# A planned two-layer transformer kernel: the planner counts the SBUF port shared by VectorE and GpSimd, the set-up is reordered, and the two-tile mixer matmuls go in four columns

## The chip, the cores and the metric

The kernel runs on one core of a Trainium2 chip. The metric is the device time of one execution in microseconds (us). Before the change the median of three runs is 1062.91 us (1060.59 to 1063.03). The engines are called as the profile calls them: PE is TensorE's matmul, PEld its weight load, DVE is VectorE, ACT is ScalarE, POOL is GpSimd, and SP is SyncE, which issues most DMAs.

## The reference, cut to what matters

There are 2048 tokens of width 448. Two layers, with the same weights, run one after the other; each adds an attention block and then a mixer block to x.

```python
def _A_ref(x, wqkv, wo):          # 16 heads of width 28
    qkv = (x @ wqkv) ...          # q, k, v
    p = _softmax(q @ k.T * Dh ** -0.5, axis=-1)
    return (p @ v) ... @ wo

def _B_ref(x, w1, w2, w3, w4):
    h = _gelu(_layernorm(x) @ w1)
    hs = (four quarters of h's columns, shifted by 1, 1, 2, 2 tokens) @ w2
    x1 = x + hs
    return x1 + _gelu(_layernorm(x1) @ w3) @ w4   # w3: 448 x 1792

x = A_x
for layer in range(2):
    x = x + _A_ref(_layernorm(x), A_wqkv, A_wo)
    x = x + _B_ref(_layernorm(x), B_w1, B_w2, B_w3, B_w4)
```

## The kernel before

**A static plan.** The order of instructions on each engine is not written by hand. Generators such as k_proj, q_proj, d_chain, t_norm, t_mixA and t_mixB yield operations, each with an engine, an assumed duration, and the tiles that it reads and writes. Sched.run simulates the engines with these durations and picks, again and again, the operation that can start first; priorities (the RANK table, the number given to spawn) decide between operations that compete for PE or DVE. The result is a fixed order on every engine, in which semaphores carry the dependences. The chip keeps the order and not the times: if an instruction takes longer on the chip than in the plan, what stands behind it on its engine waits.

**Attention.** Scores are computed in blocks of 128 keys by 512 columns (four tiles of queries for one head, or two tiles of keys for two tiles of queries). The queries are cut into chunks, CHUNKS: three of four tiles and two of two tiles in each layer; ORDER gives the pieces of the keys in which each chunk is worked through, and four groups g of four heads each run through every piece. One such pass is a segment, and ("segstart", n) is the signal that segment n begins. The scores of three blocks and of two blocks alternate in PSUM banks 0 to 2 and 3 and 4, and one ACT instruction (L1564) exponentiates three or two blocks into PT. PV, the product with v, accumulates in bank 5 (L777). Over both layers there are 2048 blocks.

**Blocks on DVE.** Some blocks bypass ACT: d_first (L1408) takes the scores out of PSUM on DVE, and d_chain makes the exponential there with a polynomial in four more instructions (L1435, L1437, L1439, L1442). t_scores looks for such a block a few rows ahead (DLO to DHI rows, or RLO to RHI for a block that takes the third bank of a unit) if a share of FTH of the planned PE time was filler (D_RATE), or if DVE's planned load is below DTH (R_RATE), if the buffers are free, and if the segment has so far taken fewer than rate x 4 x (row + 1). The rates are per layer and chunk.

**Norms.** t_norm scales the output of attention. One way goes through DRAM (three DMAs: rT, rscr, fb) and ends in a product on POOL (L1669); the other, where PENORM says so, uses small PE matmuls and ends on DVE (L1691). PENORM holds for the last chunk of layer 1 and for the fourth group of a chunk that is true in PE_NORM.

**Mixer.** t_mixA normalizes, transposes by DMA, multiplies by w1 and applies GELU with a tanh: a square on POOL (L1810), a product on DVE (L1811), tanh on ACT (L1812), a product on DVE (L1813). t_mixB does the shifted product with w2, the second norm and w3; GELU is one large ACT instruction for a group of tiles (L1989), with a table load before and after it. t_w4 multiplies by w4. mm (L777) issues one matmul; mm4 (L786) splits a matmul of up to 128 output rows into four of 32 columns of the array each, side by side. Groups of two tiles have a moving width of 256, and t_mixA and t_mixB choose mm4 only above 300. After the last exp the signal ("tail",) opens all banks, and what is left of the mixer runs to the end.

**Fillers.** Where the plan finds PE idle, keep_pe_busy inserts matmuls of an identity (L2035), which compute nothing that is used. The first may come at 6.0 us of the plan.

**Set-up.** t_load loads x and the weights; t_ln1_first normalizes the first four tiles (L964, L965, L970, L972, L979), transposes them on PE (tr_pe, L1003) and copies them to xT on DVE (L1010) or on ACT (L1011). t_pack spreads the columns of wk (on ACT, L910) and of wq (on POOL, L913, or ACT); t_squares (L921) and t_ratio estimate a ratio of weights, whose square root is a power on POOL (L939) and gives RTN (L940). The first projections k and q (k_proj, q_proj) follow, each with a sum of squares; kmaxc, bcb and bc29 (L1138, L1273, L1275) give the bias that the first q (L1176) needs before the first scores.

Of the kernel before, what the change touches and what calls it, by code (L numbers as in the profile page):

```python
# [184 lines left out]
class Sched:  # L185
# [12 lines left out]
    def __init__(self, P):  # L198
        self.P = P
        self.cur = {e: 0.0 for e in ENGS}  # L200
        self.runq = []
        self.pendq = []
        self.opq = []
        self.waiters = {}
        self.cache = {}
        self.seq = 0
        self.pe_mode = None
        self.act_tab = None
        self.events = set()
        self.evt_t = {}  # L210
        self.busy = {}
        self.res_t = {}
        self.log = []
        self.reserved = set()
        self.clock = 0.0
        self.fill = None
        self.recent = []
        self.fills = []
        self.dead = set("b%d" % i for i in range(8))
        self.bank_of = {("ps", i): "b%d" % i for i in range(8)}  # L220
# [102 lines left out]
    def keep_pe_busy(self, until):  # L323
        if self.fill is None:
            return
        if self.pe_mode is None:
            self.pe_mode = "col4"
            self.cur["pe"] = max(self.cur["pe"], 6.0)
        dur, fn, banks, key, reads = self.fill
        forced = 0  # L330
        while True:
            t = self.cur["pe"]
            self.recent = [x for x in self.recent if x[1] > t - 3.4]
# [3 lines left out]
            if not fits:  # L337
                if used > self.LOW * win - self.LCRED * max(0.0, until - t) or forced >= 2:
                    break
                forced += 1  # L340
            elif used > self.TARGET * self.WIN:
                self.cur["pe"] = t + 0.1
                continue
# [19 lines left out]
            self.pe_mode = "col4"  # L363

# [14 lines left out]
    def run(self):  # L379
        P = self.P  # L380
        while True:
# [22 lines left out]
            for t in self.opq:  # L404
# [15 lines left out]
                for ci, ((eng, dur, fn, kw), ready) in enumerate(hit[2]):  # L420
                    if ci > 0 and (self.cur[eng] > ready + 0.05 or eng in self.reserved):
                        continue
                    start = max(ready, self.cur[eng])
                    if eng == "pe":
# [68 lines left out]
            t_end = start + dur  # L493
            if dma:
                self.cur[eng] = start + kw.get("iss", 0.35)
                t_end = start + kw.get("dma_time", 3.0)
            else:
                self.cur[eng] = t_end
# [26 lines left out]
DPRIO = 2.5  # L525
DST = [('dve', 0.6), ('dve', 0.6), ('dve', 0.34), ('dve', 0.6)]
DSEG = 1
R_RATE = {(0, 0): 0, (0, 1): 0.01, (0, 2): 0, (0, 3): 0, (0, 4): 0, (1, 0): 0, (1, 1): 0.03, (1, 2): 0.01, (1, 3): 0, (1, 4): 0.04}
RLO = 5
RHI = 7  # L530
RPRIO = 1
# [3 lines left out]
DLO = 5  # L535
DHI = 7
# [31 lines left out]
def build_kernel(nc, A_x, A_wqkv, A_wo, B_x, B_w1, B_w2, B_w3, B_w4, out, n_layers=2):  # L568
# [79 lines left out]
    with st:  # L648
# [103 lines left out]
        def op(eng, dur, fn, reads=(), writes=(), **kw):  # L752
            return (eng, dur, fn, list(reads), list(writes), kw)
# [1381 lines left out]
```

## Time and profile before

| what | us |
|---|---|
| runs: median (lowest to highest) | 1062.91 (1060.59 to 1063.03) |
| the profiled execution, whole | 1059.41 |
| the profiled execution, span from first to last instruction | 1057.7 |
| ACT busy in the span | 1001.9 |
| PE busy in the span, of it fillers (L2035) | 983.3, 136.6 |
| DVE busy, POOL busy | 735.8, 327.9 |
| first exp starts (L1564) | 16.95 |
| last exp ends | about 1005 |

The span is that of one profiled execution; the 1.7 us between it and the whole lie before its first and after its last instruction. Times in the timeline count from the start of the span. In a group of instructions the columns are: line, engine, operation, out<-in, shapes, count; then busy time and the mean of one in ns; then the idle time just before them and what ended it. In the table by stretches each engine has its busy time and its number of instructions, followed by PE's granted clock (1.00 is full), the DMA share and GB/s.

### The profile page before, as it was taken

How to read it: one execution, taken by the hardware profiler on the slowest of the kernel's cores; microseconds unless marked ns; L12 is line 12 of the kernel's file. 1: busy time of each engine (PE TensorE's matmuls, PEld its weight loads, DVE VectorE, ACT ScalarE, POOL GpSimd, SP SyncE). 2: the span in 40 equal slices, each digit the busy share in tenths (PEclk: the TensorE clock that was granted, in tenths of full speed). 3: DMA queues.
4: the chain of work that ended last, by engine and by line, in shares of the span. 5: the costliest groups of instructions: out<-in, count | busy, mean ns of one | idle time of the engine just before them, and what ended most of it. 6: DMA issues, size and time to landing. Idle time of an engine off the chain costs nothing.

```text
span 1057.7 us, 34104 instructions
## 1 busy us (share of the span) xinstructions
PE 983.3 (93%) x15301; PEld 400.4 (38%) x15301; DVE 735.8 (70%) x1432; ACT 1001.9 (95%) x907; POOL 327.9 (31%) x510
## 2 busy tenths in 40 slices
PE   6999988889999999999999989898889999899998
PEld 2322333234334344444333233343323333444465
DVE  7787799794378546876377846869778575578651
ACT  7999999999999999999999999999899999999952
POOL 2344021641264014462143201103635230433230
PEclk9999999999999999999999999999999999999999
DMA  4557123111221014220033114313502030121001
GB/s 117 130 130 237 50 62 77 42 37 31 69 47 28 18 33 98 52 43 18 22 82 89 40 42 137 110 51 114 83 12 47 25 59 13 41 60 30 12 11 33
DMA packets 96642, 64.28 MB, mean 61 GB/s; under 512 B 68656, under 2 KB 85376, under 8 KB 96496
## 3 DMA queue, kind: packets, MB, share of 16 engines
q1 hardware_dynamic: 93120, 54.02, 20.3%
q0 software_dynamic: 3376, 8.09, 2.8%
q8 instruction: 120, 1.97, 0.7%
q14 instruction: 26, 0.21, 0.1%
HBM read 28.16 MB, written 16.76 MB: 42 GB/s over the span
## 4 chain that ended last, share of the span: by engine, by line
ACT 55%; PE 26%; DVE 12%; DMA 3%; POOL 3%; issue 1%; SPq 0%; DVEq 0%; POOLq 0%
ACT PT L1564 49%; PE ps L786 14%; PE ps L1326 6%; PE ps L777 5%; ACT h2T L1989 3%; DMA rT<-ub 1%; DVE PD L1442 1%; DVE fb L1435 1%; ACT fb L1812 1%; DMA fb<-rscr 1%; DVE fb L1437 1%; DVE PD L1439 1%; DVE yd L1408 1%; ACT L1989 1%; DVE vaug L1408 1%
## 5 line engine op out<-in xcount | busy, mean ns | idle before, releaser
L1564 ACT ACTIVATE PT<-ps 128x1024 bf16<-128x1024 f32 (+1 forms) x797 | 905.8, 1324 | 14.8 <-PE ps L1326 13.4
L1326 PE MATMUL ps<-qT,kT 32*128 32x512 bf16 (+1 forms) x2560 | 311.9, 341 | 30.6 <-ACT PT L1564 25.0
L777 PE MATMUL ps<-PT,vaug 128*32 128x512 bf16 (+1 forms) x2471 | 250.0, 341 | 1.0 <-DVE ub L1645 0.9
L1326 PEld LDWEIGHTS ps<-qT,kT 32*128 32x128 bf16 x2560 | 80.0, 91 | 306.0 <-ACT PT L1564 261.8
L786 PE MATMUL ps<-xT,w 128*32 128x512 bf16 (+1 forms) x2048 | 154.2, 360 | 2.3 <-DVE PD L1439 1.8
L2035 PE MATMUL ps<-ident 128*32 128x256 bf16 x3068 | 136.6, 275 | 7.8 <-DVE yd L1408 2.5
L777 PEld LDWEIGHTS ps<-PT,vaug 128*32 128x32 bf16 x2471 | 73.9, 95 | 95.4 <-issue 78.3
L2035 PEld LDWEIGHTS ps<-ident 128*32 128x32 bf16 x3068 | 84.3, 96 | 36.6 <-issue 13.8
L786 PE MATMUL ps<-w,h2T 128*32 128x448 bf16 x1288 | 87.2, 361 | 7.8 <-ACT h2T L1989 7.4
L1971 DVE CAST h2T<-ps 128x384 bf16<-128x384 f32 (+1 forms) x84 | 52.3, 623 | 60.3 <-PE ps L786 59.8
L1669 POOL TENSOR_TENSOR otn<-ub,fb 128x512 bf16<-128x512 f32 (+1 forms) x36 | 43.3, 1202 | 145.1 <-DMA fb<-rscr 139.1
L786 PEld LDWEIGHTS ps<-xT,w 128*32 128x32 bf16 x2048 | 55.0, 95 | 49.5 <-issue 25.9
L1810 POOL TENSOR_TENSOR fb<-hT 112x512 f32<-112x512 bf16 (+1 forms) x36 | 37.9, 1056 | 73.3 <-DVE hT L1793 68.7
L1113 POOL TENSOR_TENSOR sq<-kT 128x512 bf16<-128x512 bf16 (+2 forms) x32 | 31.4, 988 | 86.2 <-DVE kT L1127 84.1
L1113 POOL TENSOR_TENSOR sq<-qT 128x512 bf16<-128x512 bf16 x28 | 32.4, 1159 | 77.3 <-DVE qT L1160 69.9
L1408 DVE TENSOR_SCALAR yd<-ps 128x512 int32<-128x512 f32 x53 | 35.8, 681 | 24.7 <-PE ps L1326 24.6
L786 PEld LDWEIGHTS ps<-w,h2T 128*32 128x32 bf16 x1288 | 35.1, 97 | 37.7 <-issue 15.1
L786 PE MATMUL ps<-xT,wq_pad 128*32 128x512 bf16 x512 | 44.4, 395 | 2.4 <-DVE hT L1793 1.9
L786 PE MATMUL ps<-xT,wk_pad 128*32 128x512 bf16 (+1 forms) x512 | 44.2, 377 | 0.0
L1896 POOL TENSOR_TENSOR x_res<-x_res,x1b 128x448 f32<-128x448 f32 x32 | 39.2, 1229 | 14.5 <-DVE xn L984 14.3
L970 POOL TENSOR_SCALAR vpe<-mv 128x1 f32<-128x1 f32 (+2 forms) x21 | 6.7, 318 | 114.5 <-DVE mv L965 114.5
L1885 POOL TENSOR_SCALAR mst<-mv 128x1 f32<-128x1 f32 x32 | 9.1, 288 | 102.2 <-DVE mv L965 101.9
(190 smaller groups left out, 1335.4 us busy)
## 6 DMA issues: line engine op xcount, KB each, us to landing
uscr<-ub SPq DMA_DIRECT2D x28, 256.0 KB
ub<-uscr SPq DMA_DIRECT2D x28, 256.0 KB
fb<-rscr SPq DMA_DIRECT2D x24, 256.0 KB
xnd<-xn SPq DMA_DIRECT2D x28, 128.0 KB, 2.0
x_res<-in_A_x_dram POOLq DMA_DIRECT2D x16, 224.0 KB, 2.7
xd<-x_res SPq DMA_DIRECT2D x16, 224.0 KB, 2.7
x_res<-xd SPq DMA_DIRECT2D x16, 224.0 KB, 4.3
out_dram<-obf SPq DMA_DIRECT2D x16, 112.0 KB
```

What stands on the lines that cost most here:

```text
L777: return lambda e: e.matmul(out=out, lhsT=lhsT, rhs=rhs, start=start, stop=stop, **kw)
L786: r.append(e.matmul(out=out[c:c + w, :], lhsT=lhsT[:, c:c + w], rhs=rhs, start=start, stop=stop, tile_position=(0, c)))
L1113: return op("pool", 0.15 + NW * 0.0018, lambda e: e.tensor_tensor(out=sq[:, si, 0:NW], in0=src, in1=src, op=ALU.mult), reads=rk, writes=[( ...
L1326: yield op("pe", (0.005 + NW * 0.00042) / nc_, lambda e, i=i, kc=kc, j=j, g=g, a=a, NW=NW, bank=bank: e.matmul(out=ps[:, bank, i * NW:(i + ...
L1408: yield op("dve", c_ps(512), lambda e: e.tensor_scalar(out=y, in0=ps[:, bi(bank), :], scalar1=SCALE * L2E * FS, scalar2=-126.0 * FS, op0=A ...
L1564: yield op("act", 0.06 + n * w * 0.000833, lambda e, bk=bk, s0=s0, n=n, w=w: e.activation(out=PT[:, s0:s0 + n, 0:w], in_=ps[:, bk[0]:bk[0] ...
L1669: yield op("pool", 0.2 + NW * 0.0021, lambda e: e.tensor_tensor(out=otn[:, g, 0:NW], in0=u, in1=rb[:, 0:NW], op=ALU.mult), reads=[uk, fk], ...
L1810: yield op("pool", 0.2 + NW * 0.00165, lambda e: e.tensor_tensor(out=f, in0=z, in1=z, op=ALU.mult), reads=hk, writes=[fk])
L1896: yield op("pool", 1.2, lambda e: e.tensor_tensor(out=X, in0=X, in1=X1, op=ALU.add), reads=[xk, ("x1b", s)], writes=[xk], deps=[nop_])
L1971: ev = op("dve", c_ps(m * NW), lambda e, hr=hr, pv=pv: e.tensor_copy(out=hr, in_=pv), reads=[("ps", bi(b))], writes=hk, touch=[b])
L1989: yield op("act", c_act(len(fr_) * NW), lambda e, v=v: e.activation(out=v, in_=v, func=ACT.Gelu_apprx_tanh), reads=allk, writes=allk, tab= ...
L2035: return [e.matmul(out=ps[32 * c:32 * c + 32, bi(b), 0:256].rearrange("p (a n) -> p a n", n=128), lhsT=ident[:, 32 * c:32 * c + 32], rhs=i ...
```

## The change

The planner gets a notion of one port. op and alt mark every operation on POOL, and those on DVE that are given `two=True` (the four of d_chain, the norms L979 and L984, the two products of the tanh GELU, L1299, L1348 and the halo copies), with `port`; when such an operation is placed, after_lock moves its planned start behind the running one on the other engine. This alters planned times and so the order; it adds no instruction. The helper both would allow the square, the norm's product, the GELU square and the residual sum on DVE, except for the keys in POOLED, which now holds all four.

The set-up changes: fillers may start at 0.5 us of the plan, count twice their time before 6 us and are not limited by TARGET before 12 us; the first two parts of wq are packed on ACT and the other two on POOL after the fourth norm; t_ratio is spawned at -1; the copies of tr_pe are on DVE alone; the first k goes out of PSUM on ACT alone.

The two-tile matmuls with w1 and w3 use mm4 (above 200 instead of 300). The tables RANK (all but one entry), Q_LEAD, D_RATE, R_RATE and PE_NORM, and DPRIO, RPRIO, DLO and DHI, have new values. LSEG holds the numbers that stood in the code; GMERGE is empty.

```diff
+        self.port = {"dve": (0.0, 0.0), "pool": (0.0, 0.0)}
...
-            self.cur["pe"] = max(self.cur["pe"], 6.0)
+            self.cur["pe"] = max(self.cur["pe"], WARM)
...
+            dur = self.fill[0] * (2 if t < COLD else 1)
...
-            elif used > self.TARGET * self.WIN:
+            elif t > WARMED and used > self.TARGET * self.WIN:
...
+    def after_lock(self, eng, start, dur):
+        a, b = self.port["pool" if eng == "dve" else "dve"]
+        return max(start, b) if start + dur > a else start
...
+                    if kw.get("port"):
+                        start = self.after_lock(eng, start, dur)
...
+            if kw.get("port"):
+                self.port[eng] = (start, t_end)
...
-DPRIO = 2.5
+DPRIO = 1.5
...
-R_RATE = {(0, 0): 0, (0, 1): 0.01, (0, 2): 0, (0, 3): 0, (0, 4): 0, (1, 0): 0, (1, 1): 0.03, (1, 2): 0.01, (1, 3): 0, (1, 4): 0.04}
+R_RATE = {(0, 0): 0, (0, 1): 0.03, (0, 2): 0.01, (0, 3): 0.02, (0, 4): 0, (1, 0): 0, (1, 1): 0, (1, 2): 0, (1, 3): 0.01, (1, 4): 0}
...
-RPRIO = 1
+RPRIO = 0.5
...
-DLO = 5
-DHI = 7
+DLO = 6
+DHI = 8
...
-Q_LEAD = {(0, 1): 8, (0, 2): 7, (0, 3): 10, (1, 0): 8, (1, 1): 11, (1, 2): 3, (1, 3): 4}
-D_RATE = {(0, 0): 0.1, (0, 1): 0.055, (0, 2): 0.035, (0, 3): 0.03, (0, 4): 0.03, (1, 0): 0.025, (1, 1): 0.095, (1, 2): 0.045, (1, 3): 0.005, (1, 4): 0.045}
-PE_NORM = {(0, 0): False, (0, 1): False, (0, 2): False, (0, 3): False, (0, 4): False, (1, 0): False, (1, 1): False, (1, 2): False, (1, 3): False, (1, 4): True, (1, 5): True}
...
+Q_LEAD = {(0, 1): 10, (0, 2): 5, (0, 3): 6, (1, 0): 4, (1, 1): 8, (1, 2): 5, (1, 3): 9}
+D_RATE = {(0, 0): 0.11, (0, 1): 0.1, (0, 2): 0.07, (0, 3): 0, (0, 4): 0, (1, 0): 0.005, (1, 1): 0.105, (1, 2): 0.03, (1, 3): 0.02, (1, 4): 0}
+PE_NORM = {(0, 0): False, (0, 1): False, (0, 2): False, (0, 3): False, (0, 4): False, (1, 0): False, (1, 1): False, (1, 2): False, (1, 3): True, (1, 4): True}
...
+LSEG = (4, 7, 9)
+POOLED = ('sq', 'otn', 'z2', 'xx')
+GMERGE = {}
+WARM = 0.5
+WARMED = 12.0
+COLD = 6.0
...
         def op(eng, dur, fn, reads=(), writes=(), **kw):
+            if eng == "pool" or (eng == "dve" and kw.pop("two", False)):
+                kw["port"] = True
             return (eng, dur, fn, list(reads), list(writes), kw)
...
-            yield ("spawn", t_ratio(), 0)
+            yield ("spawn", t_ratio(), -1)
...
-                if i == 1:
+                if i == 1 or c < 2:
                     yield op("act", 0.5, lambda e, d_=d_, src=src: e.activation(out=d_, in_=src, func=ACT.Identity),
                              reads=[("pt", 4 * i + c)], writes=[((nm,), c)])
                 else:
+                    if c == 2:
+                        yield ("wait", ("xn1", 3))
...
-                             reads=[("pt", 4 * i + c)], writes=[((nm,), c)],
-                             alt=[alt("act", 0.5, lambda e, d_=d_, src=src: e.activation(out=d_, in_=src, func=ACT.Identity))])
+                             reads=[("pt", 4 * i + c)], writes=[((nm,), c)])
...
+            evacs = [("dve", c_ps2(NW), lambda e: e.tensor_scalar(out=dst, in0=ps[:, bi(b), 0:NW], scalar1=MK, scalar2=None, op0=ALU.add)),
+                     ("act", c_act(NW), lambda e: e.activation(out=dst, in_=ps[:, bi(b), 0:NW], func=ACT.Identity, bias=MK))]
+            if fast and g == 0:
+                evacs = evacs[1:]
...
             yield op(D_[0][0], D_[0][1], lambda e: e.scalar_tensor_tensor(out=q, in0=lo, scalar=E2 / E3 * FS, in1=lo, op0=ALU.add, op1=ALU.mult),
-                     reads=yk, writes=fk, urge=urge)
+                     reads=yk, writes=fk, urge=urge, two=True)
...
-                    yield op("pe", c_mm(NW), (mm4 if NW > 300 else mm)(ps[0:112, bi(b), 0:NW], w1[:, fc, 112 * grp:112 * grp + 112], xv(xt)[:, fc, 0:NW], fc == 0, fc == 3),
-                             reads=[("xT", xt), ("w1",)], writes=[("ps", bi(b))], touch=[b], mode="col4" if NW > 300 else "plain")
+                    yield op("pe", c_mm(NW), (mm4 if NW > 200 else mm)(ps[0:112, bi(b), 0:NW], w1[:, fc, 112 * grp:112 * grp + 112], xv(xt)[:, fc, 0:NW], fc == 0, fc == 3),
+                             reads=[("xT", xt), ("w1",)], writes=[("ps", bi(b))], touch=[b], mode="col4" if NW > 200 else "plain")
```

## The prediction

> **What bounds the kernel now.** I read the page first: the engines' shares, then the chain that ended last.
>
> ```profile
> PE 983.3 (93%) x15301; PEld 400.4 (38%) x15301; DVE 735.8 (70%) x1432; ACT 1001.9 (95%) x907; POOL 327.9 (31%) x510
> ACT 55%; PE 26%; DVE 12%; DMA 3%; POOL 3%; issue 1%; SPq 0%; DVEq 0%; POOLq 0%
> ```
>
> ACT is busy 1001.9 of 1057.7 us, and over half of the chain is ACT. PE's 93% holds 136.6 us of fillers (L2035), so its share misleads. Next, busy time by stretches, to see where ACT's missing 56 us lie.
>
> ```profile
> 0.00:17.00 17.00, 9.94 (x115) 4.55 (x119) 12.34 (x51) 10.64 (x15) 6.33 (x20) 1.00 0.63 180
> ...
> 200.00:300.00 100.00, 91.93 (x1393) 36.41 (x1390) 62.91 (x111) 95.32 (x83) 35.79 (x48) 0.97 0.19 46
> ...
> 700.00:800.00 100.00, 88.92 (x1287) 32.63 (x1281) 83.42 (x140) 94.53 (x87) 42.99 (x55) 1.00 0.32 70
> ...
> 1020.00:1040.00 20.00, 19.98 (x444) 11.85 (x440) 8.84 (x18) 6.87 (x14) 6.06 (x9) 1.00 0.06 20
> ```
>
> The columns of busy time are PE, PEld, DVE, ACT, POOL. Three stages: a set-up of 17 us before the first exp; about 988 us in which ACT runs exps; and, from 1005 us, when the last exp ends, a tail of 52.7 us in which PE is full and ACT waits for it. In the middle ACT's gaps over 0.15 us, added from the timeline, come to 15.0 us, most in the second and third stretch above.
>
> Third, the groups by shape, for the price of an exp.
>
> ```profile
> L1564 ACT ACTIVATE PT<-ps 128x1536 bf16<-128x1536 f32 x380 | 587.7, 1547 | 11.1 <-PE ps L1326 9.7
> L1564 ACT ACTIVATE PT<-ps 128x1024 bf16<-128x1024 f32 x416 | 460.7, 1122 | 3.8 <-PE ps L1326 3.7
> ```
>
> Five blocks cost 1547 + 1122 = 2669 ns of ACT: 0.534 us each. ACT does 380 x 3 + 416 x 2 + 1 = 1973 of the 2048 blocks; the other 75 go through DVE (L1408: 53 + 22).
>
> Last, the timelines of the set-up and of one mid gap.
>
> ```profile
> 9.63 0.58 ACT L1011 ACTIVATE xT<-ps 128x512 bf16<-128x512 bf16 x1
> 10.42 1.90 PE L786 MATMUL ps<-xT,wk_pad 128*32 128x512 bf16 x16
> 11.68 1.01 POOL L939 TENSOR_TENSOR sc<-sc,halfs 128x4 f32<-128x4 f32 x1 [1.11 <-DVE sc L938]
> 13.67 0.16 DVE L940 TENSOR_SCALAR sc<-sc 128x4 f32<-128x4 f32 x1
> 15.37 1.04 PE L786 MATMUL ps<-xT,wk_pad 128*32 128x512 bf16 x16
> 16.95 6.88 ACT L1564 ACTIVATE PT<-ps 128x1536 bf16<-128x1536 f32 x6
> ```
>
> The same 16 matmuls take 1.90 us at 10.42 and 1.04 us at 15.37: the first projections run at a slow clock. The last copy of xT waits on ACT until 9.63.
>
> ```profile
> 201.27 2.76 POOL L1669 TENSOR_TENSOR otn<-ub,fb 128x512 bf16<-128x512 f32 x1 [5.24 <-DMA fb<-rscr]
> 205.25 2.11 DVE L1811 SCALAR_TENSOR_TENSOR fb<-fb,hT 112x512 f32<-112x512 f32 x2 [2.35 <-POOL fb L1810]
> 206.79 0.63 ACT L1812 ACTIVATE fb<-fb 112x512 f32<-112x512 f32 x1 [1.60 <-DVE fb L1811]
> 208.02 1.47 PE L786 MATMUL ps<-xT,wq_pad 128*32 128x512 bf16 x12 [1.89 <-DVE hT L1793]
> ```
>
> POOL's product takes 2.76 us while DVE runs (1.27 us when nothing of DVE overlaps), so POOL's next, then DVE's, then ACT's and PE's come late. After PE's idle 1.89 us the granted clock is half for 3.4 us.
>
> **The port.** Dividing each DVE group by whether a POOL instruction overlaps it: L1437 (two SBUF inputs) takes 684 ns alone (46 of 75) and 914 ns with overlap (29, longest 1766); L1442 685 and 897; L1439 418 and 618; L1811 685 and 1169. Groups that read PSUM do not stretch: L1645 743 and 740, L1881 673 and 660. What the new plan marks as `two` is what stretches here. Over all groups DVE loses about 37 us, POOL about 30 us. Neither is the bound, so this is no gain; the gain is in what ACT waited for. ACT's gaps that I could follow back to a stretched instruction: 1.60 and 0.31 (205-210 us), 1.34, 0.32, 0.59, 0.22 (233-242 us; L1435 took 1.15 instead of 0.68), and 1.07 (735.6 us; L1439 1.16 instead of 0.42): 5.45 us. The largest, 2.45 us at 764.5, is not of this kind: DVE stood 1.98 us on the DMA rT<-ub. A plan that keeps the two apart can take 0 to 5.45 us, and a wholly new order (all RANK, Q_LEAD) can put gaps elsewhere: bounds +5 and -10. I take 5.0, as the seven gaps have one cause, which the plan now prices.
>
> **Set-up.** The ACT copy L1011 becomes a fourth DVE copy behind three that end at 8.81 (L1010, 0.415 each); the projection can start near 9.35 instead of 10.42. If early fillers make the clock full by then, its 16 matmuls take 1.04 instead of 1.90 and wq's 1.05 instead of 1.66. That brings kmaxc from 14.04 to about 11.9. But bcb also needs RTN: L940 runs at 13.67 because DVE is at kT until 13.75, though POOL's power ended at 12.69. With kT's copy on ACT, the chain from L940 (12.7) by bcb, bc29, qT (0.78) and the scores ends at about 15.0: 1.9 us earlier, bounded by 2.6 (the ratio chain, ahead by spawn -1, some 0.6 us sooner) and by a loss of 0.6 (two fillers of 0.31 us ahead of the transposes). The two wq packs moved from POOL to ACT (0.566 each) lie in ACT's idle 2.16 us before 12.37; without that cover they cost 1.1. The two left on POOL wait for the fourth norm, at 7.80; they began at 8.50 before, and behind them on POOL only the power of L939 waits, at 11.68: nothing. The page "TensorE: Matmul & The Clock Gate" of the Trainium skill (section on the HAM clock gate) speaks against counting on it: the window of about 3.4 us runs freely and the number of cold matmuls differs between runs. By it only the earlier start of the projection, 10.42 to 9.35, would be sure: about 1.0 us.
>
> Without an entry in GMERGE and with all four keys in POOLED, `both` and the new wait in t_mixB leave their instructions as they are, and LSEG holds the old numbers; the copies of tr_pe in the tail were on DVE already: nothing.
>
> **Two-tile matmuls.** 112 matmuls of w3 and 64 of w1 become four narrow ones each. Plain: 44 in 4.98 us with 0.27 for the last, 109.5 ns each. Four narrow ones of the same width are a filler: 109 ns from start to start (median). So 0 us, and 528 more instructions; less switching between kinds (about 0.2 us a visit) for at most 30 visits, in PE time that fillers cover. The page "TensorEngine Tiling (Array Packing)" (Restrictions) says that column tiling excludes fast weight load; here loads of 32 and of 128 columns both take 95 to 98 ns and overlap, so the trace speaks for 0.
>
> **Tail.** PE is full from 975 us, without fillers. PE_NORM now holds for (1,3): its fourth group leaves the DMA way (DVE copy 950.73 to POOL product 961.48: 10.75 us) for PE's (977.07 to 982.71: 5.6 us). So tiles 12 and 13 start up to 5 us sooner, and may fill the 3.83 us of fillers at 950-975. Between 0 and 3.8 I take 1.0. If RANK leaves another tile's w4 product for the tail, it costs 3.0 us (56 matmuls, 1.50 per 28).
>
> **Offloaded blocks.** D_RATE and R_RATE cap the blocks on DVE. Counted segment by segment (rate x 4 x row, whole blocks), the caps go from 164 to 160. Used were 75. Scaling use by the new cap: chunk (0,1) from row 4 on +7, (0,2) +6, (1,3) +2, against (0,4) -2, (1,1) -2, (1,2) -5.5, (1,4) -5: about 0. Bounds +20 and -25 blocks: -10.7 and +13.4 us.
>
> **Sum.** 1.9 + 5.0 + 1.0 = 7.9 us. The profiled execution took 1059.41 (its span 1057.7) and becomes 1051.5; it lies 3.5 below the median of the runs, 1062.91, which becomes 1055.0.
>
> **Rivals.** (B) The plan finds room for more blocks on DVE: 20 more, 10.7 us, 1044. For it: fillers of 8 to 9 us in each 25 us from 100 to 175. Against: half of the cap is unused, so the cap is not the limit. (C) Slower: the offload falls to some 50. The plan now lengthens DVE's and POOL's work by their exclusion, holds the y and PD buffers longer and sees fewer openings; and the raised caps, at (0,1) and (0,2), were not reached (10 of 16, 6 of 12), while lowered ones fall where blocks were used (11 in (1,2), 5 in (1,4)). Price 25 x 0.534 = 13.4: 1055.0 + 13.4 = 1068. It cancels the gain at 15 blocks fewer, and is slower beyond 0.3% from 21 fewer. (D) The change does not do what it says: chip and plan still differ elsewhere (DMA, as at 764.5), new gaps equal old ones: 1062.
>
> **How the numbers follow.** A as summed, 0.52, own range 1049 to 1060; B 0.16; C 0.23; D 0.09. A change of under 0.3%, 3.2 us, can hardly be told from none. Faster is A and B, 0.68; same D, 0.09; slower C, 0.23. The range takes in B and C with the bounds of the gaps: 1042 to 1069.
>
> **What would show it.** First exp near 15.0 us; 16 matmuls of wk in about 1.05 at the first projection; overlapped L1437 rows near 684; ACT's mid gaps 10 us or less; the first DVE step 70 to 80 times; last exp to end 50 to 53 us. Under 60 first steps, or a tail over 56 us, would make it wrong.

## The result and the profile after

The changed kernel takes 1063.05 us, median of 20 runs (1060.52 to 1066.27); the kernel before, in 20 runs beside it, 1061.21. The ratio, taken over the means without one run of the kernel before that took 4679 us, is 1.0027 with an interval of 1.0014 to 1.0039: slower by about 3 us (the medians alone are 1.8 us apart). A second measurement beside other runs (e7_after_again below) gave 1.0032 (1.0012 to 1.0051). The forecast was 1055.0 and faster; the time lies inside the range and on the other side. The profiled execution took 1063.28 us, its span 1061.5 instead of 1057.7.

Lines have moved by 25 to 30: the exp is L1591, the steps of a block on DVE are L1435, L1462, L1464, L1466 and L1469, mm4 is L811, the scores L1353, a filler L2065. First the page's engines and its chain, as before.

```profile
PE 990.9 (93%) x15980; PEld 410.0 (39%) x15983; DVE 680.6 (64%) x1365; ACT 1007.3 (95%) x913; POOL 306.0 (29%) x507
...
ACT 72%; PE 20%; DMA 3%; DVE 3%; issue 1%; SPq 1%; POOL 0%; DVEq 0%
```

DVE's share of the chain fell from 12% to 3% and POOL's from 3% to 0. The stretch fell as well: time over the median of the same shape without overlap, summed over DVE and POOL, is 39.3 us instead of 75.1. So the change does what it says, and the first half of rival D, that it does not, is out. ACT is busier by 5.4 us, though, and DVE idler by 55.2. The table by stretches shows it in the middle of the kernel (columns as before: PE, PEld, DVE, ACT, POOL).

```profile
0.00:17.00 17.00, 13.97 (x246) 7.76 (x247) 12.30 (x52) 12.41 (x17) 5.30 (x18) 1.00 0.64 181
200.00:300.00 100.00, 92.86 (x1388) 35.51 (x1380) 72.94 (x129) 97.76 (x88) 34.60 (x57) 0.98 0.25 39
700.00:800.00 100.00, 91.16 (x1290) 33.97 (x1291) 69.49 (x126) 99.60 (x91) 42.52 (x75) 1.00 0.37 75
1020.00:1040.00 20.00, 19.62 (x476) 13.30 (x468) 10.13 (x20) 3.93 (x8) 6.76 (x16) 1.00 0.08 27
```

From 700 to 800 us ACT's busy time rose from 94.53 to 99.60 while DVE's fell from 83.42 to 69.49: work went from DVE back to ACT. The groups by shape say which.

```profile
L1591 ACT ACTIVATE PT<-ps 128x1536 bf16<-128x1536 f32 x383 | 599.2, 1564 | 10.2 <-PE ps L1353 9.6
L1591 ACT ACTIVATE PT<-ps 128x1024 bf16<-128x1024 f32 x419 | 470.5, 1135 | 5.2 <-PE ps L1353 5.2
```

383 x 3 + 419 x 2 = 1987 blocks are on ACT, so 61 went through DVE, not 75. That is what rival C had forecast, at 14 fewer instead of 25; which of its two reasons held is taken up below.

The span divides into three stages. The first exp starts at 16.02 (16.95 before), the last one ends at 1008.75 (1005.07), the tail is 52.80 (52.60). The middle is thus 992.74 instead of 988.12. In it ACT does 73.1 us of other work in both kernels and is idle for 16.85 us (16.90 before); what is left for exps, each counted from its start to the next start, is 902.8 instead of 898.1. So the sum of the profiled pair is -0.9 (set-up), +4.7 (exps), 0 (idle), +0.2 (tail). The unchanged idle is the surprise, because the gaps that it consists of are not the same. Two of the new ones follow. The largest in the timeline:

```profile
79.68 0.81 POOL L856 DMA_DIRECT2D w<-in_B_w_dram  x1
...
81.02 1.12 POOL L858 DMA_DIRECT2D w<-in_B_w_dram  x1
...
86.05 7.14 SPq L1123 DMA_TRANSPOSE xT<-xnd  x1
...
95.47 0.41 PE L811 MATMUL ps<-xT,wk_pad 128*32 128x512 bf16 x4 [3.00 <-DMA xT<-xnd]
...
96.47 1.45 ACT L1591 ACTIVATE PT<-ps 128x1536 bf16<-128x1536 f32 x1 [2.93 <-PE ps L1353]
```

A transposing load of xT is issued at 86.05, some 5 us after POOL has issued the loads of the mixer's large weights w3 and w4 (L856 and L858), and SP is held in it for 7.14 us. PE waits 3.00 us, then ACT 2.93, and 0.48 and 0.68 in the next two steps: 4.1 us. Before, the order was the other way about:

```profile
74.91 2.13 SPq L1098 DMA_TRANSPOSE xT<-xnd  x1
...
83.84 0.82 POOL L831 DMA_DIRECT2D w<-in_B_w_dram  x1
```

The other comes from the one large stretch that was followed to a gap:

```profile
310.19 1.28 POOL L1696 TENSOR_TENSOR otn<-ub,fb 128x512 bf16<-128x512 f32 x1
...
311.50 3.05 DVE L1462 SCALAR_TENSOR_TENSOR fb<-yd 128x512 f32<-128x512 uint16 x1 [1.79 <-POOL otn L1696]
311.97 2.03 POOL L1837 TENSOR_TENSOR fb<-hT 112x512 f32<-112x512 bf16 x2
...
317.39 1.45 ACT L1591 ACTIVATE PT<-ps 128x1536 bf16<-128x1536 f32 x1 [2.10 <-PE ps L1353]
```

L1462 takes 3.05 us (0.69 alone) beside POOL, and an exp comes 2.10 us late. The gaps that were followed back to this cause were 5.45 us before; this one of 2.10 is the one followed back now. At 205 to 210 us, where 1.60 and 0.31 us of the old gaps lay, there is a new gap of another cause, again a transposing load, on which PE waits with the exps behind it:

```profile
206.48 0.61 PE L811 MATMUL ps<-xT,w 128*32 128x512 bf16 x8 [1.68 <-DMA xT<-xn]
...
207.46 1.94 ACT L1591 ACTIVATE PT<-ps 128x1024 bf16<-128x1024 f32 x2 [1.33 <-PE ps L1353]
```

The theory to be tested was therefore: separating the engines works and is worth some 3 us; the order that came with it loses more, by 14 blocks that are back on ACT and by one load that stands behind others. The rivals: narrow matmuls cost PE time after all; the set-up loses; the accounting itself costs more than the stretch that it avoids.

### The profile page after: what moved, and what is told of

It is laid out like the page before. It is cut to its first block, busy times and chain, and to the rows that moved or that the text cites. A ratio compares the mean times of both kernels' runs of the same rounds, so it can differ in the third digit from the quotient of the medians.

```text
span 1061.5 us, 35381 instructions
## 1 busy us (share of the span) xinstructions
PE 990.9 (93%) x15980; PEld 410.0 (39%) x15983; DVE 680.6 (64%) x1365; ACT 1007.3 (95%) x913; POOL 306.0 (29%) x507
## 4 chain that ended last, share of the span: by engine, by line
ACT 72%; PE 20%; DMA 3%; DVE 3%; issue 1%; SPq 1%; POOL 0%; DVEq 0%
ACT PT L1591 66%; PE ps L811 11%; PE ps L1353 4%; PE ps L802 3%; ACT h2T L2019 2%; DMA xT<-xnd 2%; ACT fb L1839 1%; PE ps L2065 1%; ACT L2019 1%; DMA xT<-xn 1%; ACT L1591 1%; DVE fb L1462 0%; DMA rT<-ub 0%; DMA PT<-in_A_wqkv_dram 0%; SPq L1015 0%
## 5 line engine op out<-in xcount | busy, mean ns | idle before, releaser
L1591 ACT ACTIVATE PT<-ps 128x1024 bf16<-128x1024 f32 (+1 forms) x802 | 910.4, 1340 | 15.5 <-PE ps L1353 14.8
L1353 PE MATMUL ps<-qT,kT 32*128 32x512 bf16 (+1 forms) x2560 | 315.2, 341 | 36.8 <-ACT PT L1591 28.4
L1353 PEld LDWEIGHTS ps<-qT,kT 32*128 32x128 bf16 x2560 | 80.6, 91 | 317.6 <-ACT PT L1591 285.1
L811 PE MATMUL ps<-xT,w 128*32 128x512 bf16 (+4 forms) x2368 | 160.9, 345 | 5.8 <-DMA xT<-xn 4.0
L2065 PE MATMUL ps<-ident 128*32 128x256 bf16 x3212 | 145.9, 279 | 4.2 <-DVE hT L1820 2.4
L2065 PEld LDWEIGHTS ps<-ident 128*32 128x32 bf16 x3212 | 90.8, 98 | 31.9 <-issue 13.1
L811 PE MATMUL ps<-w,h2T 128*32 128x448 bf16 x1288 | 90.5, 358 | 5.7 <-ACT h2T L2019 5.7
L811 PEld LDWEIGHTS ps<-xT,w 128*32 128x32 bf16 (+1 forms) x2368 | 64.6, 96 | 50.1 <-issue 27.2
L811 PEld LDWEIGHTS ps<-w,h2T 128*32 128x32 bf16 x1288 | 36.0, 97 | 34.9 <-issue 15.2
L811 PE MATMUL ps<-xT,wk_pad 128*32 128x512 bf16 (+2 forms) x576 | 44.6, 366 | 3.1 <-DMA xT<-xnd 3.0
L1435 DVE TENSOR_SCALAR yd<-ps 128x512 int32<-128x512 f32 x43 | 29.5, 687 | 25.6 <-PE ps L1353 25.2
L811 PE MATMUL ps<-wo_pad,otn 128*32 128x448 bf16 x512 | 39.5, 356 | 2.9 <-DVE x_res L1750 1.6
L811 PE MATMUL ps<-w,hT 112*32 112x448 bf16 x512 | 41.2, 355 | 0.5 <-DVE x1b L1908 0.5
L811 PE MATMUL ps<-xT,wq_pad 128*32 128x512 bf16 x448 | 39.3, 388 | 1.4 <-DMA xT<-xnd 0.9
```

The source lines that it names most:

```text
L811: r.append(e.matmul(out=out[c:c + w, :], lhsT=lhsT[:, c:c + w], rhs=rhs, start=start, stop=stop, tile_position=(0, c)))
L1353: yield op("pe", (0.005 + NW * 0.00042) / nc_, lambda e, i=i, kc=kc, j=j, g=g, a=a, NW=NW, bank=bank: e.matmul(out=ps[:, bank, i * NW:(i + ...
L1435: yield op("dve", c_ps(512), lambda e: e.tensor_scalar(out=y, in0=ps[:, bi(bank), :], scalar1=SCALE * L2E * FS, scalar2=-126.0 * FS, op0=A ...
L1591: yield op("act", 0.06 + n * w * 0.000833, lambda e, bk=bk, s0=s0, n=n, w=w: e.activation(out=PT[:, s0:s0 + n, 0:w], in_=ps[:, bk[0]:bk[0] ...
L2065: return [e.matmul(out=ps[32 * c:32 * c + 32, bi(b), 0:256].rearrange("p (a n) -> p a n", n=128), lhsT=ident[:, 32 * c:32 * c + 32], rhs=i ...
```

## The experiments

All are timed beside runs of the kernel before. "Before" and "changed" name the two kernels of the case.

**e1_before_fill: the kernel before with the early fillers alone.**

```diff
-            self.cur["pe"] = max(self.cur["pe"], 6.0)
+            self.cur["pe"] = max(self.cur["pe"], WARM)      # 0.5
```

> The kernel before with the early fillers alone (WARM, WARMED, COLD); everything else of the order stays as before. Theory (the early fillers are what the set-up gained, through the clock): the clock is full by about 7 us instead of 13.4, the 16 matmuls of the first wk projection take about 1.05 us instead of 1.90, the first exp starts 0.9 to 1.6 us before 16.95, and the whole gets shorter by as much: about 1 us. Rival (the gain of 0.94 us came from the changed order and the fillers only stand in the way of the transposes): the first exp at 16.9 or later, no gain.

Measured: 1057.97 us, ratio 0.9979 (0.9961 to 0.9996). The timeline of its set-up shows no gain there. In the profile ACT's idle in the middle is 14.9 us instead of 16.9, with the same order on ACT, DVE and POOL as before; what brings the 0.2% stays open.

```profile
11.18 1.90 PE L811 MATMUL ps<-xT,wk_pad 128*32 128x512 bf16 x16
...
14.58 0.66 DVE L1165 TENSOR_REDUCE kmaxc<-ps 128x1 f32<-128x512 f32 x1
...
17.46 1.44 ACT L1591 ACTIVATE PT<-ps 128x1536 bf16<-128x1536 f32 x1
```

The clock was full from 6.66 us, but half again from 10.1 to 13.5, so the first 16 matmuls took 1.90 us as before, and the first exp came 0.5 us later than before: the theory fell and the rival's first exp "at 16.9 or later" came, though not its "no gain". In this run early fillers alone did not secure the clock at the first projection. In the profiled execution of the changed kernel it did stay full, from 6.99 us; in another execution of that kernel (e7_after_again) it became full at 4.24. The page "TensorE: Matmul & The Clock Gate" of the Trainium skill (section on the HAM clock gate) says that the window runs freely, and these two times of one kernel agree with it.

**e2_after_nomm4: the changed kernel with wide two-tile matmuls.**

```diff
-(mm4 if NW > 200 else mm)
+(mm4 if NW > 300 else mm)
```

> The changed kernel with the two-tile matmuls of w1 and w3 as one wide matmul each, as before the change; the rest of the order is as in the changed kernel. Theory (the loss is not in these matmuls): the time is that of the changed kernel within 1 us, the tail 52 to 54 us. Rival (four times as many instructions slow a full PE, above all between 975 us and the end): 2 to 4 us faster than the changed kernel, most of it in the tail.

Measured: 1066.92 us, 1.0059 (1.0041 to 1.0076). It isn't faster but some 3 us slower than the changed kernel's 1.0027 and 1.0032. The two traces lie 4.0 us apart at the last exp. Of this 2.5 us arise before 487 us, where neither kernel has reached such a matmul and the order on ACT, DVE and POOL is the same: so much one execution can differ from another. The other 1.5 us arise after it. So the narrow matmuls are no cost. A gain of 1 to 3 us goes with them, but it isn't shown to be theirs, because from 488 us on the plan also orders DVE's work differently.

**e3_before_noblocks: the kernel before with no block on DVE.**

```diff
-R_RATE = {... (1, 1): 0.03, (1, 2): 0.01, (1, 3): 0, (1, 4): 0.04}
+R_RATE = {(L, c): 0 for L in (0, 1) for c in range(5)}
```

(and D_RATE in the same way)

> The kernel before with all D_RATE and R_RATE at 0: no block is exponentiated on DVE, all 2048 on ACT. The price of a block: my prediction took 0.534 us from the mean durations, which gives 40 us more between the first and the last exp; from the starts of 24 exps in 27.52 us it is 0.455, which gives 34 us. If the blocks on DVE also made the gaps on ACT (through stretched DVE and POOL instructions), the gaps of 16 us shrink as well and it is less, 22 to 30 us. Tail unchanged at 50 to 55.

Measured: 1089.19 us, 1.0273 (1.0253 to 1.0293): 0.0273 of some 1060 us is 28.9, or 0.39 us for each of 75 blocks. In the profile the exps' time (middle less idle less other work) is 929.9 instead of 898.1: 31.8 / 75 = 0.424 us. The whole rose by less than the exps and the 9.0 us of other work that ACT now has in the middle, because ACT's idle fell by 5.2 us and the tail by 6.3 (to 46.35; 50 to 55 was expected). The prediction paid 0.534. The groups and the timeline show why.

```profile
L1564 ACT ACTIVATE PT<-ps 128x1536 bf16<-128x1536 f32 x410 | 635.4, 1550 | 8.4 <-PE ps L1326 7.7 <-PE ps L777 0.3
L1564 ACT ACTIVATE PT<-ps 128x1024 bf16<-128x1024 f32 x409 | 461.1, 1127 | 1.3 <-PE ps L1326 1.1
```

```profile
60.03 18.31 ACT L1564 ACTIVATE PT<-ps 128x1536 bf16<-128x1536 f32 x16
```

By the means, 8 of each shape are 8 x (1.550 + 1.127) = 21.4 us; back to back they took 18.31. An exp begins before the one ahead of it has ended, by some 0.2 us, and a mean duration counts that time twice. 18.31 / 40 = 0.458 us a block. Over the whole middle it is much the same: the exps' time by the number of blocks on ACT is 0.455 us before, 0.454 in the changed kernel and 0.454 here. So 14 blocks are 5.4 to 6.4 us by these prices; in the pair of traces it is 4.7.

**e4_after_oldsetup_fill: the changed kernel with the old set-up order, early fillers kept.** t_ratio is spawned at 0, wq's four parts may go to POOL, the first k is not kept on ACT; the copies of tr_pe stay on DVE alone:

```diff
-            yield ("spawn", t_ratio(), -1)
+            yield ("spawn", t_ratio(), 0)
...
-                if i == 1 or c < 2:
+                if i == 1:
...
-            if fast and g == 0:
+            if False:
```

> The changed kernel with the old set-up order (ratio chain at 0, wq packed as before, first k on DVE or ACT as before), but with the early fillers. Theory (spawning the ratio chain at -1 put its matmuls, which wait 0.87 us for ACT, ahead of the transposes, and cost what the clock had gained): first exp 0.3 to 1.0 us earlier than the 16.02 of the changed kernel, whole time shorter by as much. Rival (the new order is worth its 0.9 us): first exp at 16.5 to 17.0 and 0.5 to 1 us slower than the changed kernel.

Measured: 1064.43 us, 1.0036 (1.0021 to 1.0050), first exp at 16.46 (16.02 in the changed kernel, 15.87 in e7_after_again). The theory, an earlier first exp, fell. The new order is worth 0.4 to 0.6 us in the traces and is no loss.

**e5_after_lateweights and e7_after_again: the changed kernel with the weights of the mixer loaded later, and the changed kernel itself on the same chip.** LSEG holds the segments at whose start the loads begin.

```diff
-LSEG = (4, 7, 9)
+LSEG = (4, 9, 11)
```

> The changed kernel with LSEG = (4, 9, 11): the loads of wo, w1, w2 wait for segment 9 instead of 7, those of w3 and w4 for segment 11 instead of 9; the rest of the order is the changed kernel's. In the changed kernel's trace the transposed load of xT at 86.05 us stands behind w3 and w4 (issued at 79.7 to 82.1): its issue takes 7.14 us instead of 2.13, and ACT then stands 2.93 + 0.48 + 0.68 = 4.1 us. Theory (the new order of RANK moved that load from 74.9 us, ahead of the weights, into them, and this is a part of the loss): the issue takes 2 to 3 us, these gaps vanish, 3 to 4.5 us faster than the changed kernel. Rival (the order there is short of time whatever the load does, as the clock is cold and other work is late): less than 1 us faster.

> The changed kernel itself beside the others of this call, so that they can be compared on the same chip. As before the call: 0.1 to 0.4% slower than the kernel before. For the two-tile matmuls: e2, without them, was 1.0059 of before; if they are worth something, this one is below 1.0041; if what e2 showed was chance, above it.

Measured: 1059.85 us against 1063.49, so 3.64 us less; against before 1.0000 (0.9981 to 1.0019). The timeline of e5_after_lateweights:

```profile
84.05 26.38 ACT L1591 ACTIVATE PT<-ps 128x1536 bf16<-128x1536 f32 x23
...
85.52 2.26 SPq L1123 DMA_TRANSPOSE xT<-xnd  x1
...
100.11 0.81 POOL L856 DMA_DIRECT2D w<-in_B_w_dram  x1
```

The transposing load takes 2.26 us again, and ACT runs 23 exps without a gap through the place of the 2.93 us. The load behind w3 and w4 costs 3.6 us, and without it the change makes no difference that can be measured.

**e6_before_port: the kernel before with the port counted in the plan, nothing else.**

```diff
+                    if kw.get("port"):
+                        start = self.after_lock(eng, start, dur)
```

> The kernel before with the port in the planner alone: op marks POOL and `two`, after_lock delays; all tables, the set-up and the two-tile matmuls as before. Theory (planning the port removes stretched instructions, but what it is worth is small, and the tables decide the time): the stretch of DVE and POOL together, 75 us before and 39 us in the changed kernel, falls below 50 us with about as many blocks on DVE (74); ACT's gaps behind stretched instructions fall from 5.45 to under 2.5 us; the time does not follow, since an order with the old ranks leaves more of the mixer to the tail: tail 58 to 65 us instead of 52.6, whole 5 to 12 us slower than before. Rival (the port was what cost time, and the new tables are what lost it): tail as before, whole 3 to 6 us faster than before.

Measured: 1066.38 us, 1.0064 (1.0044 to 1.0084), with 74 blocks on DVE and a stretch of 54.4 us instead of 75.1; the expected drop below 50 was missed. The tail grew to 56.35, less than the 58 or more expected, ACT's idle in the middle to 19.66, and the first exp starts at 18.06. The accounting alone, with tables that were chosen without it, is a loss of 7 us, and it costs one block.

**e11_after_noport: the changed kernel without the port's wait.**

```diff
-        return max(start, b) if start + dur > a else start
+        return start
```

> The changed kernel without the new wait in the planner: everything else of the change, its tables included, stays, and only the line of after_lock returns the start unaltered. The planned length becomes 1054.7 instead of 1044.15 with 62 blocks on DVE instead of 61. Theory (a plan that doesn't count the port is run 21 us or more late, one that counts it 14 to 17 us late; what a plan is worth is set by its tables, which were chosen with the port counted): a span of 1073 to 1080, 11 us or more above the changed kernel, with a stretch of DVE and POOL of 55 us or more. Rival (the accounting is what costs the change its time, since it holds buffers longer): 1062 or less, and 5 blocks or more beyond 61.

Measured: 1093.73 us, 1.0316 (1.0286 to 1.0346), beyond what the theory expected, and by another way: the stretch is 44.7 us and not 55 or more. The rival fell too: 62 blocks are on DVE, one beyond 61. ACT's idle in the middle is 38.7 us. Its largest gap in the timeline is the load again:

```profile
86.61 1.12 POOL L858 DMA_DIRECT2D w<-in_B_w_dram  x1
...
89.97 6.93 SPq L1123 DMA_TRANSPOSE xT<-xnd  x1
...
105.42 1.02 ACT L1591 ACTIVATE PT<-ps 128x1024 bf16<-128x1024 f32 x1 [7.29 <-PE ps L1353]
```

Here ACT loses 7.29 us at one place; the rest of the loss was not taken apart. With e6_before_port this shows that tables and accounting can't be valued apart: each way of mixing them is slower than either kernel. It does not show what the accounting is worth.

**e8_port_newtables, e9_port_newtables_late and e10_noport_newtables: both planners with tables chosen anew.** For the first and the second the port is counted, for the third it isn't; in each the tables RANK, Q_LEAD, D_RATE, R_RATE and PE_NORM have values that make the plan shorter. The second also has LSEG = (4, 9, 11). The first two have the new set-up and the narrow two-tile matmuls, the third the old set-up and the wide ones.

> The changed kernel with other values in RANK, Q_LEAD, D_RATE, R_RATE and PE_NORM, chosen so that the plan with the port counted sends 74 blocks through DVE instead of 61 and is 8.2 us shorter (planned length 1035.9 instead of 1044.15). Theory (the port's accounting is sound, the change's loss lies in the order that came with it: 14 blocks fewer at some 0.38 us and one load issued too late): the chip follows this plan as it followed the other, 14 to 17 us longer than planned, so a span of 1050 to 1053.5 and a whole of 1052 to 1055, 8 to 11 us under the changed kernel; overlapped stretch of DVE and POOL, 39.3 us in the changed kernel and 75.1 before, stays between 38 and 55 with the blocks back. Rival (separating the engines costs what it saves, whatever the tables): within 4 us of the changed kernel, 1059 or more, with the 74 blocks there.

> As e8_port_newtables, with the weights of the mixer loaded later (LSEG 4, 9, 11 instead of 4, 7, 9); 75 blocks planned on DVE, planned length 1036.5. Theory of the load behind the weights: in the new order, too, the transposed load of the first mixer tile stands behind w3 and w4 if these are issued ahead of it; if the profile of e8_port_newtables shows that load at 5 us or more, this kernel is 2 to 4 us faster than that one, otherwise within 2 us of it. Rival: the later loads collide elsewhere, 2 us or more slower.

> The kernel before with other values in the same tables (no port counted, old set-up, plain two-tile matmuls), chosen by the same kind of search for the shortest plan: 89 blocks on DVE instead of 75, planned length 1027.6 instead of 1035.06. Theory (a plan that doesn't count the port is longer on the chip by 21 to 24 us): a span of 1049 to 1052, no better than e8_port_newtables although its plan is 8 us shorter; stretch of DVE and POOL 80 us or more, since there are more blocks. Rival (the port's stretch is hidden mostly and only the number of blocks counts): 14 blocks more at 0.38 us and 2 us of other gain, a span under 1048, faster than e8_port_newtables by 3 us or more.

Measured, on one chip: 1051.81 us, 0.9919 (0.9895 to 0.9943); 1049.27 us, 0.9906 (0.9881 to 0.9930); 1065.18 us, 1.0060 (1.0038 to 1.0082). The first two are the fastest of the study, 7 and 10 us faster than the kernel before beside them; the median of e8_port_newtables lies just below the 1052 to 1055 that the theory expected. Its profiled execution is the fastest of its six, 1048.18 us with a span of 1046.4. The page:

```profile
PE 977.9 (93%) x15543; PEld 399.1 (38%) x15543; DVE 712.1 (68%) x1428; ACT 998.1 (95%) x914; POOL 310.1 (30%) x507
...
ACT 77%; PE 16%; DMA 3%; DVE 3%; SPq 1%; issue 1%; DVEq 0%
```

74 blocks are on DVE again, at a stretch of 42.6 us: both at once can be had. ACT's idle in the middle is 12.0 us. The transposing load takes 4.94 us there, just under the 5 us of the expectation, and 3.73 with the later weights, where w1 and w2 stand right ahead of it. By its own condition the expectation was then "within 2 us"; the medians are 2.5 us apart, and the profiled spans (1046.4 and 1047.4) 1.0 the other way. This settles nothing about the load. In e10_noport_newtables 89 blocks are on DVE, the stretch is 78.8 us, and ACT's idle is 25.9. Its chain and a place of its timeline:

```profile
ACT 43%; PE 37%; DVE 16%; issue 1%; DMA 1%; POOL 1%; SPq 0%; DVEq 0%; POOLq 0%
```

```profile
440.81 3.18 DVE L1838 SCALAR_TENSOR_TENSOR fb<-fb,hT 112x512 f32<-112x512 f32 x1
...
441.70 1.05 POOL L1138 TENSOR_TENSOR sq<-qT 128x512 bf16<-128x512 bf16 x1
...
442.71 0.72 POOL L1696 TENSOR_TENSOR otn<-ub,fb 128x256 bf16<-128x256 f32 x1
...
444.71 1.04 PE L811 MATMUL ps<-xT,wq_pad 128*32 128x512 bf16 x8 [2.50 <-DVE qT L1187]
...
446.34 1.45 ACT L1591 ACTIVATE PT<-ps 128x1536 bf16<-128x1536 f32 x1 [1.68 <-PE ps L1353]
```

The product L1838 takes 3.18 us (0.67 alone in this shape) while POOL runs; the qT behind it on DVE comes late, PE waits 2.50 us and ACT 1.19 and 1.68. So the rival, that only the number of blocks counts, fell: 15 more blocks made the kernel slower by 13 us than e8_port_newtables. How far the two differ by the port, by the set-up and the two-tile matmuls (some 1 us and 1 to 3 us by the runs above), and by the luck of two orders, one kernel of each kind can't say. The theory's other half, that the chip runs behind a plan by a set amount, fell as well: by the medians, less the 1.7 us outside the span, the kernels are longer than planned by 14 us in e8_port_newtables and by 23 in the run below with the port counted, and by 36 in e10_noport_newtables and 37 in e11_after_noport without.

**e12_after_oldrrate: the changed kernel with two entries of R_RATE as before.**

```diff
-(1, 1): 0, ... (1, 4): 0}
+(1, 1): 0.03, ... (1, 4): 0.04}
```

> The changed kernel with two entries of R_RATE as they were before: (1, 1) 0.03 and (1, 4) 0.04, both 0 in the change; D_RATE and all else stay. The prediction scaled the use of DVE by the caps of both tables together; if it is R_RATE's own gate (DVE's planned load) that let the blocks in (1, 1) and (1, 4) through, these two entries alone bring 10 to 13 of the 14 lost blocks back, and exps then take some 4 us less in chunks (1, 1) and (1, 4). Theory (a block in the last chunk is not free: its DVE steps stand in the way of the mixer that must be done by the end): the last exp ends earlier by 3 to 5 us against the changed kernel after 475 us, but the tail grows by 3 to 7 us, so the whole is within 3 us of the changed kernel or slower. Rival (the lost blocks are the loss by themselves): 4 us or more faster than the changed kernel, with a tail under 54 us.

Measured: 1073.36 us, 1.0133 (1.0113 to 1.0154). 73 blocks are on DVE, 12 of the 14. By the plan, eight more are in (1,1), seven more in (1,4), and three fewer in (1,0). But neither the theory's way nor the rival's came. The profiled execution is the slowest of five, 1078.82 us. In it the exps take 2.3 us less than in the changed kernel, ACT's idle is longer by 16.1 us, and the last exp ends at 1022.49, 13.7 later. The largest gap is one of the order:

```profile
686.13 0.39 PE L1353 MATMUL ps<-qT,kT 32*128 32x512 bf16 x3
...
686.46 2.91 PE L811 MATMUL ps<-xT,wk_pad 128*32 128x384 bf16 x56
...
692.60 0.60 PE L1353 MATMUL ps<-qT,kT 32*128 32x512 bf16 x5
...
693.16 2.37 ACT L1591 ACTIVATE PT<-ps 128x1024 bf16<-128x1024 f32 x2 [5.15 <-PE ps L1353]
```

Between the scores at 686.13 and those at 692.60 PE's order holds a projection of 56 matmuls and what depends on it; ACT stands 5.15 us. Here the blocks that came back cost more than they brought, in an order that was not chosen for them.

## Why the prediction was wrong, step by step

**Offloaded blocks: the step that failed.** The prediction scaled the use by the caps of D_RATE and R_RATE taken together, chunk by chunk, and arrived at "about 0". It was -14. A block passes by either of two gates: planned filler (D_RATE) or DVE's planned load (R_RATE). Counted in the two plans by gate, and by the chunk that a block belongs to:

| chunk | before: D_RATE + R_RATE | changed: D_RATE + R_RATE | forecast | change |
|---|---|---|---|---|
| (0,1) | 10 + 3 | 6 + 6 | +7 | -1 |
| (0,2) | 6 + 0 | 8 + 4 | +6 | +6 |
| (1,1) | 8 + 7 | 5 + 0 | -2 | -10 |
| (1,2) | 7 + 4 | 7 + 0 | -5.5 | -4 |
| (1,3) | 2 + 0 | 0 + 4 | +2 | +2 |
| (0,4) and (1,4) | 4 + 4 | 0 + 0 | -7 | -8 |
| the other three | 20 + 0 | 17 + 4 | 0 | +1 |
| all | 57 + 18 | 43 + 18 | about 0 | -14 |

Two chunks, (0,1) and (1,1), were off by 8 each. In both the cap of D_RATE rose (16 to 28 and 28 to 32 blocks) and D_RATE let fewer through (10 to 6 and 8 to 5). Of D_RATE's caps, 132 and 136 in all, 57 and 43 were used; of R_RATE's, 32 and 24, it was 18 and 18. So a cap of D_RATE is not what limits its blocks, and the sum of both caps hid that. In (1,1) R_RATE went to 0 and seven blocks with it; in e12_after_oldrrate, with its entries for (1,1) and (1,4) back, R_RATE lets nine through in (1,1) and seven in (1,4). Why D_RATE's gate opened less often in the new order, no run takes apart.

Rival C gave two reasons. The one on the caps held (raised ones that were not reached, lowered ones that were in use). The other, that the plan sees fewer openings once it counts the port, fell: counting it with the old tables left 74 blocks of 75 (e6_before_port), and leaving it out with the new ones gave 62 instead of 61 (e11_after_noport). The prediction's sign of being wrong, under 60 first steps, did not show at 61.

**The price of a block** was 0.534 us from mean durations and measures 0.33 (the pair of traces) to 0.46 (exps back to back). With the right count the term would have been +7.5 by the old price; the pair of traces has +4.7. In e12_after_oldrrate the 12 blocks that came back took only 2.3 us off the exps.

**Port gaps: mechanism right, sum wrong.** Forecast -5.0; the gaps followed back to that cause fell by 3.4, and stretched time by 36 us (75.1 before by the count above, not the 37 + 30 of the prediction), of which a part belongs to the 14 missing blocks (with no block at all, in e3_before_noblocks, the stretch is 32.6). The prediction named the other bound, "a wholly new order can put gaps elsewhere", and priced it at nothing in the sum. That is the second step that failed, and the largest such gap was the load behind the weights, 3.6 us by e5_after_lateweights. With the gap behind the other transposing load at 207 us and smaller ones, ACT's idle stayed at 16.85 us where 10 or less was forecast. This is rival D's second half, "new gaps equal old ones", which had a chance of 0.09. For the new order the prediction looked up no transfer: the weights are issued by POOL at a segment's start, the transposing load by SP when its rows are written, and nothing keeps the one behind the other when all ranks change.

**Set-up:** forecast -1.9 and the first exp at 15.0; measured -0.9 and 16.02. The profile of the changed kernel's set-up:

```profile
8.33 0.61 ACT L947 ACTIVATE PT<-wk_pad 128x512 bf16<-128x512 bf16 x1
...
8.85 1.02 ACT L935 ACTIVATE wq_pad<-PT 128x448 bf16<-128x448 bf16 x2
...
9.00 0.25 PE L802 MATMUL ps<-ones_bf,PT 128*128 128x1 bf16 x4 [0.74 <-ACT PT L947]
...
9.11 0.55 PE L1029 MATMUL ps<-ident,xn 128*128 128x128 bf16 x7
...
9.78 0.61 ACT L947 ACTIVATE fb<-wq_pad 128x512 bf16<-128x512 bf16 x1
...
10.63 0.61 PE L811 MATMUL ps<-xT,wk_pad 128*32 128x512 bf16 x8
...
12.21 1.01 POOL L965 TENSOR_TENSOR sc<-sc,halfs 128x4 f32<-128x4 f32 x1 [2.60 <-DVE sc L964]
...
13.14 0.69 DVE L1165 TENSOR_REDUCE kmaxc<-ps 128x1 f32<-128x512 f32 x1 [1.02 <-PE ps L811]
...
13.75 0.16 DVE L966 TENSOR_SCALAR sc<-sc 128x4 f32<-128x4 f32 x1
...
16.02 2.36 ACT L1591 ACTIVATE PT<-ps 128x1536 bf16<-128x1536 f32 x2
```

Two assumptions failed. The transposes stand behind the ratio's matmuls in PE's order, and these wait 0.74 us for ACT, so the projection starts at 10.63 and not at 9.35. And the two packs of wq that moved to ACT (L935, 1.02 us) were said to lie in idle time; they lie ahead of the second square (L947 at 9.78), on which the ratio waits. POOL's power starts at 12.21 instead of 11.68 and ends at 13.22; by then DVE is at kmaxc, and RTN's L966 follows at 13.75, not at 12.7. kmaxc itself, which bcb needs as well, starts at 13.14 and not at the 11.9 of the forecast, as the projection ahead of it is late. Before it was

```profile
14.04 0.69 DVE L1138 TENSOR_REDUCE kmaxc<-ps 128x1 f32<-128x512 f32 x1
```

so it came 0.90 us sooner, and the first exp 0.93. What was right is the clock: the wk matmuls take 0.61 + 0.61 us instead of 1.90.

**Two-tile matmuls:** forecast 0, with the measured loads against the rule of the page "TensorEngine Tiling (Array Packing)" (Restrictions); e2_after_nomm4, with the wide ones, is 1 to 3 us slower. So whatever the rule costs, the narrow form was no loss here.

**Tail:** forecast -1.0, measured +0.2, just outside its bounds of 0 and -3.8.

**The sum** with the measured terms: -0.9 set-up, +4.7 blocks, -3.4 port gaps, +4.1 load (2.93 + 0.48 + 0.68), -0.7 other gaps (the rest, old and new together, as the idle is unchanged), +0.2 tail: +4.0 against the +3.8 of the spans. Against the forecast of -7.9 the blocks are 4.7 us of the miss, the idle that did not fall 5.0, the set-up 1.0 and the tail 1.2.

## What to carry to other kernels

When a planned kernel's tables change, count by gate and not by cap what each will let through, and check every transfer that several engines order against each other, because the gaps that a better model removes come back where the new order was not looked at. Price work on an engine by a run of it back to back, not by the mean duration of its instructions. A better cost model and the tables that were chosen under the old one have to be changed together: against the kernel before, the model alone lost 7 us, the change's tables without it 35, newly chosen tables without it 6, and the model with newly chosen tables gained 7 to 10 (the second and the last with the new set-up and the narrow matmuls). How much of that is the model's and how much the luck of an order is not shown.

## What the runs showed of the hardware that was not expected

- **Overlap on ACT.** Sixteen exps whose mean durations add up to 21.4 us ran in 18.31.
- **Which DVE work stretches.** In the changed kernel L1464 takes 685 ns alone (53) and 808 overlapped (8), L1462 685 and 883, L1469 685 and 848, and L1466, one tensor input, 419 and 642; L1672, which reads PSUM, takes 745 and 747. The page "SBUF — State Buffer" of the Trainium skill (section on the two separate sides) calls the shared port an exclusive lock on which the loser blocks; the longest agree with that: of the nine instructions over 1.4 us on L1462, L1464, L1469 and L1838 in the changed kernel, seven end 0.55 us (0.548 to 0.553) after the last POOL instruction beside them, as if they had run after it; and two or three POOL instructions in a row hold DVE for all of them (3.05 us at 311.50, 3.18 us at 440.81 in e10_noport_newtables).
- **A transposing load is slow behind a large load.** The same load took 2.13 and 2.26 us with w3 and w4 issued after it, and 7.14, 6.93 and 4.94 with them issued before. With the smaller w1 and w2 issued some 2 us ahead of it, it took the 2.26 in e5_after_lateweights and 3.73 in e9_port_newtables_late.
- **One kernel's runs differ by its granted clock.** In the 29 runs of the kernel before beside e5_after_lateweights the span went from 1053.7 us at a mean clock of 0.998 to 1065.2 at 0.987. PE is busy for 93% of the span, and still single stretches of 3.4 us run at half clock, 3 of them in the profiled execution before and 5 in the one after. The three profiled executions with the most idle on ACT in the middle (25.9, 38.7 and 32.9 us in e10_noport_newtables, e11_after_noport and e12_after_oldrrate) also have the lowest clocks, 0.978, 0.975 and 0.976; all others have 0.990 to 0.995. Which of the two brings the other is not shown.
